# Two-layer MLP after attention on one core: the first block's first part with plain products, token operands made in the last group of the part before, bank evictions ahead of weights

## The chip, the cores and the metric

The kernel runs on one core of a Trainium2 chip. The metric is device time in microseconds (us) of one execution. TensorE (PE in the profile) multiplies, ScalarE (ACT), VectorE (DVE) and GpSimd (POOL) do elementwise work, SyncE (SP) issues the DMA transfers.

## The reference, cut to what matters

Causal attention with a decay comes first (4 batches, 8 heads, 576 tokens of 64 values). Its output, 2304 tokens of 512 values, goes through two gated layers:

```python
def _moe_ref(x, w_gate, w_val, w_out, rms_g):          # 512 -> 1536 -> 512
    rms = np.sqrt(np.mean(x * x, axis=-1, keepdims=True) + 1e-06)
    xn = x / rms * rms_g
    g = xn @ w_gate
    silu = g * (1.0 / (1.0 + np.exp(-g)))
    val = xn @ w_val
    return silu * val @ w_out

def _moe2_ref(x, w_in, w_out):                         # 512 -> 2048 -> 512
    h = x @ w_in
    g = h * (1.0 / (1.0 + np.exp(-h)))
    return g @ w_out
```

The weights arrive as 64-bit floats, the tokens as 32-bit floats, and the result is 32-bit.

## The kernel before

Attention is the same in both kernels. It ends with a normalisation of the tokens, which are kept in SBUF in the buffer `xa`, features on the partitions. Behind it come layer **a** (gate, val, out) and layer **b** (in, out). Each runs over two parts of the tokens: part 0 has 1280 tokens (two tiles of 512 and a rest of 256), part 1 has 1024 (two tiles of 512). The stages below are called a0, a1, b0 and b1.

Every 32-bit product is made of three matmuls on TensorE, since both operands are split into a rounded high part and a remainder (`terms`: high x high, high x low, low x high). A split is one copy on ScalarE (names that end in `h`: `wh`, `b11h`, `hh`) and one subtraction on VectorE (`wl`, `b11l`, `hl`).

A stage is a loop over groups of two hidden blocks of 128 (six groups in layer a, eight in layer b). A group does the following:

- It loads each weight matrix's two blocks (`unit_in`). In part 0 they come as raw 64-bit words (`st`) and are converted by one ScalarE and four VectorE operations (lines 128 to 132), and a copy of the result is kept in DRAM; in part 1 that copy is read back (`f<-kepta`).
- It multiplies by seven products instead of eight (Strassen's scheme over 2 x 2 blocks: two feature halves and two token tiles, `Products`): p1, p2, p6, p5, p7, p4, p3, each of 6 matmuls of 512 columns, so 42 per weight matrix. The weight sums that it needs are made on POOL (line 147), and the token operands are `b11`, `b21`, `t2`, `t1`, `t3`, `t4`, `b22`. In part 0 the 256 `rest` tokens follow at the end, as plain products (24 matmuls of 256 columns per matrix).
- The finished sums are taken out of the PSUM banks by `copy` (line 632, ScalarE, tile `c`) and `plus` (line 636, VectorE); gate and val are multiplied, split (`hh`, `hl`) and wait for the output product.
- The output product of a group (`second1` at line 742, `second2` at line 759) runs inside the next group, between the products, and adds its banks (`s`) into `xa`.

The token operands are made by `prepare(ph)` (lines 583ff.), which is called at the head of a part's first group: four differences on POOL (line 588, 128x1024 each, in the weight buffers `f`), seven or eight splits on ScalarE and VectorE (lines 579 and 580).

What order an engine's instructions have is decided by a scheduler from the order of the code, its dependences and the hint in `spread`, which lets a group's weight work start behind a marked instruction of the group before. The pools bound how far anything runs ahead: four `wh`/`wl` buffers, two `st` and two `f`, eight `c` tiles, two `s` and six `t` banks. Each engine runs its instructions in the order that came out, so one that waits holds those behind it.

## Time and profile before

| | |
|---|---|
| median of 3 runs | 1115.4 us (1111.41 to 1116.17) |
| the profiled execution | 1112.8 us, of which its span 1111.0 us |
| busy: PE, DVE, ACT, POOL | 1044.0, 803.7, 600.6, 413.2 us (94, 72, 54, 37% of the span) |
| mean granted TensorE clock | 0.972 |
| chain of work that ended last | PE 63%, DVE 17%, ACT 7%, POOL 6%, issue 5%, DMA 2% |
| costliest groups off PE | POOL `f` line 147 120.1 us, DVE `wl` line 151 99.8, DVE `hl` line 580 98.0, DVE `xa` line 759 86.6 |

The span runs from the first to the last instruction of one profiled execution; the time has some 2 us more around it. A matmul's own duration in the profile overlaps the next one's, so what a matmul costs is read from the distance of starts in a stretch without waits.

### The profile page before, as it was taken

To read this page: it belongs to the slowest core of one execution; us is meant where nothing else is said; L and a number is where in the kernel's file an instruction comes from. 1 tells how busy PE (TensorE), PEld (TensorE's weight loads), DVE (VectorE), ACT (ScalarE), POOL (GpSimd) and SP (SyncE) were. 2 spreads that over 40 slices of the span, in tenths; PEclk is the share of its full clock that TensorE was granted. 3 is DMA by queue.
4 is the path that set the end of the run, shared out by engine and by line. 5 is a ranking of instruction groups with operands and counts; after the bars stand their busy time and mean duration, and the time that the engine had idled before them with its cause. 6 is when DMAs were issued, how large, how long until landed. Compare 5 with 4: busy or idle time off the path is not lost.

```text
span 1111.0 us, 15986 instructions
## 1 busy us (share of the span) xinstructions
PE 1044.0 (94%) x5403; PEld 847.2 (76%) x5403; DVE 803.7 (72%) x1540; ACT 600.6 (54%) x1215; POOL 413.2 (37%) x631
## 2 busy tenths in 40 slices
PE   8998999968999999997999999799999999999998
PEld 7766778746787787785778888578888877888887
DVE  7788787866777888866546568877888897456664
ACT  7888888755554444443454344465454555544441
POOL 7766667503224214226423433422122243221310
PEclk9989999987999999998999999899999998999999
DMA  6644333110425225221111111133333313311202
GB/s 139 172 132 106 86 87 89 31 58 1 137 90 171 86 86 171 76 67 42 63 48 48 58 58 57 46 126 123 123 125 125 124 45 101 108 39 51 71 13 76
DMA packets 108402, 95.92 MB, mean 86 GB/s; under 512 B 62256, under 2 KB 83152, under 8 KB 108320
## 3 DMA queue, kind: packets, MB, share of 16 engines
q1 hardware_dynamic: 108320, 94.89, 28.2%
q8 instruction: 43, 0.70, 0.3%
q14 instruction: 39, 0.32, 0.1%
HBM read 72.25 MB, written 22.62 MB: 85 GB/s over the span
## 4 chain that ended last, share of the span: by engine, by line
PE 63%; DVE 17%; ACT 7%; POOL 6%; issue 5%; DMA 2%; POOLq 0%; SPq 0%; DVEq 0%; ACTq 0%
PE t L621 25%; PE s L621 23%; PE s L406 5%; PE t L429 4%; PE o L457 3%; POOL f L147 3%; DVE wl L151 3%; POOL f L588 2%; ACT wh L150 2%; DVE hl L580 1%; DVE c L131 1%; DVE xa L759 1%; PE s L365 1%; DVE c L636 1%; DMA f<-kepta 1%
## 5 line engine op out<-in xcount | busy, mean ns | idle before, releaser
L147 POOL TENSOR_TENSOR f<-f 128x256 f32<-128x256 f32 x160 | 120.1, 772 | 319.5 <-DVE f L132 85.7
L162 POOL TENSOR_TENSOR wol<-c,woh 128x512 fp32r<-128x512 f32 x56 | 74.9, 1348 | 214.3 <-ACT woh L161 210.7
L151 DVE TENSOR_TENSOR wl<-f,wh 128x1024 fp32r<-128x1024 f32 x80 | 99.8, 1256 | 55.1 <-ACT wh L150 55.1
L580 DVE TENSOR_TENSOR hl<-c,hh 128x512 fp32r<-128x512 f32 x140 | 98.0, 705 | 55.4 <-ACT hh L579 54.3
L632 ACT ACTIVATE c<-t 128x512 f32<-128x512 f32 x120 | 69.9, 590 | 101.0 <-PE t L621 100.0
L150 ACT ACTIVATE wh<-f 128x1024 fp32r<-128x1024 f32 x80 | 79.3, 999 | 72.1 <-POOL f L147 56.3
L636 DVE TENSOR_TENSOR c<-t,c 128x512 f32<-128x512 f32 x120 | 81.6, 686 | 49.6 <-ACT c L632 32.7
L621 PE MATMUL s<-woh,hh 128*128 128x512 f32 x290 | 114.1, 393 | 2.4 <-DVE xa L759 2.4
L579 ACT ACTIVATE hh<-c 128x512 fp32r<-128x512 f32 x140 | 81.4, 584 | 62.7 <-POOL c L713 44.5
L621 PE MATMUL s<-wol,hh 128*128 128x512 f32 x290 | 113.1, 390 | 0.0
L621 PE MATMUL s<-woh,hl 128*128 128x512 f32 x290 | 113.0, 390 | 0.0
L759 DVE TENSOR_TENSOR xa<-s,xa 128x512 f32<-128x512 f32 (+1 forms) x127 | 86.6, 682 | 32.6 <-PE s L621 32.1
L706 ACT ACTIVATE c<-c 128x512 f32<-128x512 f32 x84 | 52.8, 629 | 94.5 <-DVE c L636 94.5
L621 PE MATMUL s<-hh,woh 128*128 128x512 f32 (+1 forms) x240 | 90.3, 376 | 12.1 <-DVE xa L742 12.1
L393 POOL TENSOR_SCALAR dt<-ncb,c8t 128x64 f32<-128x64 f32 (+2 forms) x144 | 79.4, 553 | 41.2 <-DVE nm L409 32.7
L621 PE MATMUL s<-hl,woh 128*128 128x512 f32 (+1 forms) x240 | 89.4, 373 | 0.2 <-DVE hl L580 0.2
L621 PE MATMUL s<-hh,wol 128*128 128x512 f32 (+1 forms) x240 | 89.4, 373 | 0.0
L421 ACT ACTIVATE pr<-pr,nm 128x192 f32<-128x192 f32 (+3 forms) x144 | 80.1, 556 | 16.1 <-DVE nm L409 11.0
L409 DVE CUSTOM_DVE_ANT_0 pr<-s,dt 128x64 f32<-128x64 f32 (+7 forms) x160 | 70.2, 451 | 20.5 <-PE s L406 7.7
L742 DVE TENSOR_TENSOR xa<-s,xa 128x512 f32<-128x512 f32 (+1 forms) x100 | 62.4, 633 | 20.8 <-PE s L621 20.8
L429 PE MATMUL t<-ident,pr 128*128 128x128 f32 x384 | 72.2, 289 | 3.3 <-ACT pr L421 1.6
L621 PEld LDWEIGHTS s<-woh,hh 128*128 128x128 f32 x290 | 54.7, 189 | 17.2 <-DVE xa L759 6.6
(190 smaller groups left out, 2781.3 us busy)
## 6 DMA issues: line engine op xcount, KB each, us to landing
st<-in_moe_w_out_dram SPq DMA_DIRECT2D x28, 512.0 KB, 3.7
st<-in_moe_w_in_dram SPq DMA_DIRECT2D x16, 512.0 KB, 3.8
st<-in_moe_w_gate_dram SPq DMA_DIRECT2D x12, 512.0 KB, 3.9
kepta<-f SPq DMA_DIRECT2D x24, 256.0 KB, 2.2
st<-in_moe_w_val_dram SPq DMA_DIRECT2D x12, 512.0 KB, 3.9
f<-kepta SPq DMA_DIRECT2D x24, 256.0 KB, 2.6
out_dram<-xa SPq DMA_DIRECT2D x17, 256.0 KB, 2.0
ncb<-nc8d SPq DMA_DIRECT2D x30, 144.0 KB, 3.1
```

Of the source, the lines that this page charges most:

```text
L147: nc.gpsimd.tensor_tensor(out=out_, in0=x, in1=y, op=op)
L150: nc.scalar.activation(out=hi[i][:, u], in_=f[i][:, u], func=AF.Copy)
L151: nc.vector.tensor_tensor(out=lo[i][:, u], in0=f[i][:, u], in1=hi[i][:, u].bitcast(F32), op=ALU.subtract)
L162: nc.gpsimd.tensor_tensor(out=lo, in0=f, in1=hi.bitcast(F32), op=ALU.subtract)
L393: nc.gpsimd.tensor_scalar(out=dt, in0=p.nct[:, :n], scalar1=c8t[:, c, p.i : p.i + 1], scalar2=1.0, op0=ALU.add, op1=ALU.mult)
L421: e = nc.scalar.activation(out=pr, in_=pr, func=AF.Exp, bias=self.nm, scale=-1.0, accum_out=p.batch.sums[:, self.c, p.hp : p.hp + 1])
L429: nc.tensor.transpose(pt[:, jj * P : (jj + 1) * P], pr[:, jj * P : (jj + 1) * P], ident)
L579: nc.scalar.activation(out=hi, in_=src, func=AF.Copy)
L580: nc.vector.tensor_tensor(out=lo, in0=src, in1=hi.bitcast(F32), op=ALU.subtract)
L621: nc.tensor.matmul(ps, lhsT=l, rhs=r, start=start and z == 0, stop=stop and z == len(mms) - 1, skip_group_check=not (start and stop))
L636: nc.vector.tensor_tensor(out=t, in0=ps, in1=t, op=ALU.add)
L759: nc.vector.tensor_tensor(out=a, in0=ps, in1=a, op=ALU.add)
```

## The change

Five edits:

1. Layer a's part 0 multiplies plainly (`unit_plain`, `block`): for each 128 hidden units 12 matmuls of 512 columns per token tile, so 48 per weight matrix and group where there were 42. No weight sums are made, one tile holds both blocks of a matrix, and the low half of the weights is made on POOL. The buffers `b11`, `b21`, `t4`, `b22` hold the plain halves of the two token tiles there.
2. `prepare` gives back its pieces one by one. For the three later parts they are issued in the last group of the part before, each behind the product that last used the buffer it overwrites (`coming`), in pieces of 128x512; the differences go into `c` tiles. The first part's splits are written straight behind attention.
3. The evictions of the banks (`copy`, `plus`, `put`, the additions into `xa`) are put 600 places ahead in the scheduler's order.
4. In b0 the products of the 256 rest tokens are done behind p2 and behind p7 instead of at the end of the group.
5. In b0 the second half of the weights' low part goes to POOL, and the `c` ring has nine tiles instead of eight.

```diff
+AHEAD = 600
...
         for i in range(2):
             u = slice(0 if plain or not i else 1, 4)
             nc.scalar.activation(out=hi[i][:, u], in_=f[i][:, u], func=AF.Copy)
-            nc.vector.tensor_tensor(out=lo[i][:, u], in0=f[i][:, u], in1=hi[i][:, u].bitcast(F32), op=ALU.subtract)
+            (nc.gpsimd if plain and i else nc.vector).tensor_tensor(out=lo[i][:, u], in0=f[i][:, u], in1=hi[i][:, u].bitcast(F32), op=ALU.subtract)
...
+    def unit_plain(w, key, m):
+        w, s = words(w)
+        hi, lo = wip.tile([P, 4, G2], F32R, tag="wh", name="wh"), wip.tile([P, 4, G2], F32R, tag="wl", name="wl")
+        f = plain_half()
+        for i in range(2):
+            weights(f[:, 2 * i : 2 * i + 2].rearrange("p a f -> p (a f)"), w[:, s * (m + i) * P : s * (m + i + 1) * P], s * P, (key, m + i))
+        nc.scalar.activation(out=hi, in_=f, func=AF.Copy)
+        nc.gpsimd.tensor_tensor(out=lo, in0=f, in1=hi.bitcast(F32), op=ALU.subtract)
...
+        def diff(nm, u, v):
+            t[nm] = [tmp.tile([P, TT], F32, tag="c", name="c") for _ in range(2)]
+            for o, u_, v_ in zip(t[nm], u, v):
+                nc.gpsimd.tensor_tensor(out=o, in0=u_, in1=v_, op=ALU.subtract)
+        def parts_(nm, src):
+            for c in range(2):
+                split(xs[nm][0][:, c], xs[nm][1][:, c], src[c])
+        def p6():
+            diff("t1", b[0, 1], b[0, 0])
+            diff("t2", b[1, 1], t["t1"])
+            parts_("t2", t["t2"])
...
         def copy(ps):
             t = tmp.tile([P, TT], F32, tag="c", name="c")
-            nc.scalar.activation(out=t, in_=ps, func=AF.Copy)
+            with tc.high_priority(offset=AHEAD):
+                nc.scalar.activation(out=t, in_=ps, func=AF.Copy)
             return t
...
+        if plain:
+            where = [[(xs[nm], c) for nm in pr for c in range(2)] for pr in (("b11", "b21"), ("t4", "b22"))]
+            where.append([(xs["rest"], c) for c in range(NCC)])
+            def block(n, i, j):
+                w = TT if j < 2 else CUT - 2 * TT
+                ps = bank(pst)[:, :w]
+                terms(ps, [(win[n][i][c], [t[:, c_] for t in x]) for c, (x, c_) in enumerate(where[j])], True, True)
+                put(n, (i, j), ps, w)
+            return [(f"tile{j}" if i else "", [_p(block, n, i, j) for n in range(len(win))]) for j in (0, 1, 2) for i in range(2)]
...
-            order += [_p(s.rest, i) for i in range(2) for s in sets]
+            order.insert(5, ("rest", [_p(s.rest, 1) for s in sets]))
+            order.insert(2, ("", [_p(s.rest, 0) for s in sets]))
...
-            if g == 0:
-                prepare(ph)
+            coming = prepare(parts_left.pop(0)) if g + G >= NF and parts_left else {}
...
+            for nm, ps in order:
+                for p in ps:
+                    p()
+                for fn in todo[: 2 if len(ps) == 2 else 1 + (len(todo) > 7)]:
+                    fn()
+                    todo.remove(fn)
+                coming.pop(nm, int)()
...
+    parts_left = [1, 0, 1]
+    for j, names in enumerate((("b11", "b21"), ("t4", "b22"))):
+        for i, nm in enumerate(names):
+            for c in range(2):
+                split(xs[nm][0][:, c], xs[nm][1][:, c], xparts[0][:, 2 * i + c, j * TT : (j + 1) * TT])
...
     for ph in range(2):
-        layer("a", [w_gate, w_val], w_o1, second1, ph)
+        layer("a", [w_gate, w_val], w_o1, second1, ph, ph == 0)
```

Line numbers of the changed kernel are higher: the conversion's VectorE lines 129 to 132 are its 131 to 134, the split's 580 is 593, the addition into `xa` is 798 in layer a (742 before) and 816 in layer b (759), the multiplication of gate and val 760 (713).

First place: VectorE at the end of attention. In the kernel before, the sums of squares (`u`, line 282, then `ms`, line 286) stand between the last conversion steps of two output-weight blocks (`c_4078`, `c_4092`).

```order
L131 SCALAR_TENSOR_TENSOR c_4078<-st_4079,c_4078 128x512
L130 TENSOR_SCALAR c_4092<-c_4092 128x512
L132 SCALAR_TENSOR_TENSOR c_4078<-st_4079,c_4078 128x512
L282 TENSOR_TENSOR u_3915<-s_3909,r_3902 128x4x4 x2
L282 TENSOR_TENSOR u_3915<-s_3909,r_3902 64x4 x2
L131 SCALAR_TENSOR_TENSOR c_4092<-st_4093,c_4092 128x512
L284 TENSOR_TENSOR u_3915<-u_3915,r_3902 128x40
L132 SCALAR_TENSOR_TENSOR c_4092<-st_4093,c_4092 128x512
L286 TENSOR_REDUCE ms_3916<-u_3915 128x5
```

In the changed kernel the rows from the last scaling of the tokens (line 340) on are these, with the conversion of the same two blocks (`c_4080`, `c_4094`):

```order
L340 SCALAR_TENSOR_TENSOR xa_60<-xa_60,gcol_96,s_3973 128x288
L593 TENSOR_TENSOR b11l_3991<-xa_60,b11h_3990 128x512 x2
L593 TENSOR_TENSOR b21l_3993<-xa_60,b21h_3992 128x512 x2
L593 TENSOR_TENSOR t4l_4001<-xa_60,t4h_4000 128x512 x2
L593 TENSOR_TENSOR b22l_4003<-xa_60,b22h_4002 128x512 x2
L593 TENSOR_TENSOR restl_4011<-xa_60,resth_4010 128x512 x2
L131 TENSOR_SCALAR c_4080<-c_4080 128x512
L131 TENSOR_SCALAR c_4094<-c_4094 128x512
L132 TENSOR_SCALAR c_4080<-c_4080 128x512
L132 TENSOR_SCALAR c_4094<-c_4094 128x512
L133 SCALAR_TENSOR_TENSOR c_4080<-st_4081,c_4080 128x512
```

The conversion has moved from ahead of the normalisation to behind the first part's splits, which are one run now.

Second place: VectorE where one group of a0 follows another. Before, the second matrix's raw conversion (`f_5524`, `f_5525`) of the next group, the additions of output banks `s` and the remainder of the weights (`wl`) stand like this:

```order
L129 TENSOR_SCALAR f_5524<-f_5524 128x512
L129 TENSOR_SCALAR f_5525<-f_5525 128x512
L580 TENSOR_TENSOR hl_5485<-c_5468,hh_5484 128x256
L130 TENSOR_SCALAR f_5524<-f_5524 128x512
L130 TENSOR_SCALAR f_5525<-f_5525 128x512
L131 SCALAR_TENSOR_TENSOR f_5524<-st_5526,f_5524 128x512
L131 SCALAR_TENSOR_TENSOR f_5525<-st_5535,f_5525 128x512
L132 SCALAR_TENSOR_TENSOR f_5524<-st_5526,f_5524 128x512
L132 SCALAR_TENSOR_TENSOR f_5525<-st_5535,f_5525 128x512
L742 TENSOR_TENSOR xa_60<-s_5598,xa_60 128x512
L742 TENSOR_TENSOR xa_60<-s_5606,xa_60 128x512
L151 TENSOR_TENSOR wl_5521<-f_5524,wh_5520 128x1024
```

In the changed kernel, at the like place:

```order
L760 TENSOR_TENSOR c_5495<-t_5497,c_5495 128x512
L131 TENSOR_SCALAR f_5778<-f_5778 128x512
L798 TENSOR_TENSOR xa_60<-s_5515,xa_60 128x512
L593 TENSOR_TENSOR hl_5512<-c_5495,hh_5511 128x512
L798 TENSOR_TENSOR xa_60<-s_5523,xa_60 128x512
L132 TENSOR_SCALAR f_5778<-f_5778 128x512
L131 TENSOR_SCALAR f_5778<-f_5778 128x512
L133 SCALAR_TENSOR_TENSOR f_5778<-st_5779,f_5778 128x512
L132 TENSOR_SCALAR f_5778<-f_5778 128x512
L134 SCALAR_TENSOR_TENSOR f_5778<-st_5779,f_5778 128x512
L133 SCALAR_TENSOR_TENSOR f_5778<-st_5788,f_5778 128x512
L134 SCALAR_TENSOR_TENSOR f_5778<-st_5788,f_5778 128x512
```

The additions (line 798) stand among the steps of the conversion instead of behind all eight of them (`f_5778` is one tile of two blocks, so its rows come twice), and no `wl` follows, since it is made on POOL.

Third place: VectorE where b1 follows b0. Before, in the first group of b1, the additions of output banks (line 759), the token operands (`b11l`, `b21l`, `t1l`) and the weights' remainders (`wl`) stand in this order:

```order
L636 TENSOR_TENSOR c_9608<-t_9626,c_9608 128x512
L759 TENSOR_TENSOR xa_60<-s_9639,xa_60 128x512
L580 TENSOR_TENSOR b11l_3997<-xa_60,b11h_3996 128x1024
L759 TENSOR_TENSOR xa_60<-s_9647,xa_60 128x512
L580 TENSOR_TENSOR hl_9636<-c_9608,hh_9635 128x512
L151 TENSOR_TENSOR wl_9795<-f_9798,wh_9794 128x1024
L759 TENSOR_TENSOR xa_60<-s_9663,xa_60 128x512
L151 TENSOR_TENSOR wl_9797<-f_9799,wh_9796 128x768
L580 TENSOR_TENSOR b21l_3999<-xa_60,b21h_3998 128x1024
L759 TENSOR_TENSOR xa_60<-s_9678,xa_60 128x512
L580 TENSOR_TENSOR t1l_4003<-f_9824,t1h_4002 128x1024
```

In the changed kernel the same operands stand in the last group of b0:

```order
L816 TENSOR_TENSOR xa_60<-s_9571,xa_60 128x512
L593 TENSOR_TENSOR b11l_3991<-xa_60,b11h_3990 128x512
L816 TENSOR_TENSOR xa_60<-s_9579,xa_60 128x512
L593 TENSOR_TENSOR hl_9568<-c_9536,hh_9567 128x512
L593 TENSOR_TENSOR b11l_3991<-xa_60,b11h_3990 128x512
L593 TENSOR_TENSOR b21l_3993<-xa_60,b21h_3992 128x512 x2
L816 TENSOR_TENSOR xa_60<-s_9610,xa_60 128x512
L153 TENSOR_TENSOR wl_9767<-f_9770,wh_9766 128x1024
L153 TENSOR_TENSOR wl_9769<-f_9771,wh_9768 128x768
L816 TENSOR_TENSOR xa_60<-s_9626,xa_60 128x512
L593 TENSOR_TENSOR t2l_3995<-c_9638,t2h_3994 128x512
L593 TENSOR_TENSOR t2l_3995<-c_9639,t2h_3994 128x512
```

The token operands come in pieces of half the size, one group earlier, with the additions (line 816) between them.

## Rows read from the trace of the kernel before

**Rows 1.** Chain that ended last, in order of time: start, us, engine, line.

```profile
345.55 2.72 PE s L621 x12
356.43 1.43 PE s L621 x12
```

**Rows 2.** Eight stretches: us, busy of PE, PEld, DVE, ACT, POOL; clock, DMA.

```profile
251.06:295.20 44.14, 38.00 (x160) 30.47 (x160) 32.28 (x45) 21.20 (x33) 15.17 (x10) 0.85 0.14 45
295.20:459.10 163.90, 155.43 (x809) 130.92 (x807) 131.33 (x213) 75.95 (x130) 43.73 (x48) 1.00 0.35 114
459.10:540.00 80.90, 69.05 (x310) 56.21 (x311) 52.52 (x66) 32.52 (x48) 36.81 (x31) 0.92 0.24 78
540.00:660.86 120.86, 118.64 (x523) 96.41 (x522) 69.62 (x89) 54.93 (x86) 43.77 (x45) 1.00 0.14 44
660.86:736.60 75.74, 66.08 (x287) 53.09 (x285) 59.45 (x82) 35.89 (x56) 29.54 (x23) 0.95 0.24 77
736.60:877.41 140.81, 139.05 (x660) 114.87 (x661) 114.87 (x190) 76.98 (x135) 29.11 (x31) 1.00 0.36 117
877.41:940.00 62.59, 58.60 (x265) 48.19 (x266) 54.52 (x69) 33.95 (x54) 26.28 (x21) 0.95 0.26 86
940.00:1107.74 167.74, 167.67 (x745) 138.73 (x743) 98.00 (x131) 71.74 (x119) 35.61 (x38) 1.00 0.19 62
```

**Rows 3.** The same columns, for layer a's first stretch and one later group.

```profile
251.06:257.80 6.74, 6.51 (x16) 4.59 (x16) 6.74 (x9) 2.72 (x3) 2.14 (x1) 0.50 0.01 2
375.50:417.30 41.80, 39.34 (x204) 33.17 (x204) 34.29 (x57) 18.08 (x30) 11.20 (x13) 1.00 0.34 113
```

**Rows 4.** What PE waited for, 240 to 1111 us: total, times, longest.

```profile
PE t L621 <- ACT c L632: 13.1, 4, 5.9
PE s L621 <- DVE xa L742: 12.1, 7, 4.2
PE t L621 <- ACT wh L150: 11.7, 8, 3.4
```

**Rows 5.** PE's timeline where it waits: start, us, instruction, idle before and releaser.

```profile
265.30 0.79 PE L621 MATMUL t<-t2h,wh 128*128 128x512 f32 x1 [3.63 <-ACT c L632]
...
375.93 0.50 PE L621 MATMUL s<-hh,woh 128*128 128x512 f32 x1 [1.28 <-DVE xa L742]
...
378.77 0.50 PE L621 MATMUL t<-b11h,wh 128*128 128x512 f32 x1 [1.17 <-ACT wh L150]
...
527.43 0.72 PE L621 MATMUL s<-hh,woh 128*128 128x512 f32 x1 [4.17 <-DVE xa L742]
...
700.64 0.80 PE L621 MATMUL t<-t4h,wh 128*128 128x512 f32 x1 [5.90 <-ACT c L632]
```

**Rows 6.** VectorE's timeline at the end of attention.

```profile
240.08 1.60 DVE L131 SCALAR_TENSOR_TENSOR c<-st,c 128x512 int32<-128x512 int32 x1
...
241.71 0.69 DVE L132 SCALAR_TENSOR_TENSOR c<-st,c 128x512 int32<-128x512 int32 x1
...
243.16 1.27 DVE L297 TENSOR_TENSOR z<-y 128x5 f32<-128x5 f32 x1
...
244.86 0.17 DVE L297 TENSOR_TENSOR z<-y 128x5 f32<-128x5 f32 x1
```

**Rows 7.** PE's timeline behind it, up to layer a's first product.

```profile
246.78 0.74 PE L318 MATMUL s<-identr,rt 128*16 128x128 f32 x5 [7.04 <-DVE rt L309]
```

**Rows 8.** VectorE's timeline in the first group of b1: token operands.

```profile
912.85 1.21 DVE L580 TENSOR_TENSOR b21l<-xa,b21h 128x1024 fp32r<-128x1024 f32 x1
...
914.59 2.78 DVE L580 TENSOR_TENSOR t1l<-f,t1h 128x1024 fp32r<-128x1024 f32 x1
```

**Rows 9.** Groups by shape: weight splits and token differences; count, busy, mean ns.

```profile
L151 DVE TENSOR_TENSOR wl<-f,wh 128x1024 fp32r<-128x1024 f32 x60 | 74.0, 1242 | 53.2 <-ACT wh L150 53.2
...
L150 ACT ACTIVATE wh<-f 128x1024 fp32r<-128x1024 f32 x60 | 62.6, 1052 | 68.6 <-POOL f L147 54.4 <-PE t L621 14.2
...
L588 POOL TENSOR_TENSOR f<-xa 128x1024 f32<-128x1024 f32 x8 | 19.9, 2488 | 9.4 <-DVE wl L151 5.3 <-DVE t2l L580 2.5 <-DVE xa L327 1.4
```

More of the change, by code (lines that the diff above doesn't have):

```diff
@@ L653, in p2 @@
                 self.product(ps, "a12", "b21", True, True)
[L654 removed]
+                put(self.n, (0, 0), plus(ps, self.u1), TT)
             def p6(self):
@@ L719, in layer @@
             todo, pending[:] = list(pending), []
-            order = group(win, out_, ph == 0)
-            per = len(w_ins)
-            for i, p in enumerate(order):
-                p()
-                if i % per == per - 1:
-                    for fn in todo[: 2 if per == 2 else 1 + (len(todo) > 7)]:
-                        fn()
-                        todo.remove(fn)
+            order = group(win, out_, ph == 0, plain)
+            if plain and coming:
+                for nm in ("p6", "p5", "p7"):
+                    coming.pop(nm)()
+                coming = dict(tile0=[coming[nm] for nm in ("p1", "p2")], tile1=[coming[nm] for nm in ("p4", "p3")])
+                coming = {nm: _p(lambda fns: [fn() for fn in fns], fns) for nm, fns in coming.items()}
+            for nm, ps in order:
[5 more added lines that the diff above has]
+                coming.pop(nm, int)()
+            for fn in coming.values():
+                fn()
             for fn in todo:
@@ L738, in block @@
             a = xparts[ph][:, o, t : t + w]
-            if first:
-                nc.scalar.activation(out=a, in_=ps, func=AF.Copy)
-            else:
-                nc.vector.tensor_tensor(out=a, in0=ps, in1=a, op=ALU.add)
+            with tc.high_priority(offset=AHEAD):
+                if first:
+                    nc.scalar.activation(out=a, in_=ps, func=AF.Copy)
+                else:
+                    nc.vector.tensor_tensor(out=a, in0=ps, in1=a, op=ALU.add)
         return [_p(block, o) for o in range(NCC)]
@@ L755, in block @@
                 a = accs[ph][:, t // P + s, cs]
-                if first:
-                    nc.scalar.activation(out=a, in_=ps, func=AF.Copy)
-                else:
-                    nc.vector.tensor_tensor(out=a, in0=ps, in1=a, op=ALU.add)
+                with tc.high_priority(offset=AHEAD):
+                    if first:
+                        nc.scalar.activation(out=a, in_=ps, func=AF.Copy)
+                    else:
+                        nc.vector.tensor_tensor(out=a, in0=ps, in1=a, op=ALU.add)
                 if last:
```

68 lines of the change are left out of this document (35 added, 33 removed).

## The prediction

> **What bounds the kernel now.** I read the chain that ended last first: in the layers it runs for long pieces from PE to PE, so TensorE sets the time there, and every gap in PE's row is time. Its unwaited pieces give the price of a matmul by the distance of starts: 12 of 512 columns take 2.72 us, 0.2267 each, and 12 of 256 columns 1.43 us, 0.119 each [rows 1].
>
> Then I cut the layers, from the first product at 251.06 us to the end of the last at 1107.74, into eight stretches [rows 2]. In the trace they hold 3114 matmuls of 512 columns (1680 in products, 1434 in outputs) and 636 of 256. At the prices above that is 705.9 + 75.7 = 781.6 us, and the stretches last 856.7, so 75.1 us are lost. Each stretch's length less its own matmuls gives the place (wide and narrow counted in each): first group of a0 44.1 - 30.9 (111 and 48) = **13.3**; rest of a0 163.9 - 151.9 (519 and 288) = **12.0**; from a0 to a1 80.9 - 61.2 (226 and 84) = **19.7**; a1 120.9 - 116.8 (509 and 12) = **4.0**; from a1 to b0 75.7 - 62.0 (261 and 24) = **13.7**; b0 140.8 - 136.7 (540 and 120) = **4.1**; from b0 to b1 62.6 - 54.9 (217 and 48) = **7.7**; b1 167.7 - 167.1 (731 and 12) = **0.6**. The reader is to see that steady a1 and b1 run at PE's pitch already, and that four places where a part begins lose 54 of the 75.
>
> What ends the waits says why. PE waited 13.1 us in four pieces for a copy of a bank (line 632), 12.1 us for the addition into `xa` (line 742), 11.7 us for the weights' high half (line 150) [rows 4]. At three part starts the wait is 3.63, 4.17 and 5.90 us [rows 5]: VectorE and ScalarE there hold the token splits and the raw conversion, and what empties PSUM queues behind them. The rest of the loss is slow clock: from 251.06 to 257.80 the granted clock is 0.50, the 1.2 GHz level, and the stretches with long waits have a mean of 0.85 to 0.95 [rows 2, 3]. So a gap costs again behind itself, and a gap that goes gives that back.
>
> **The change, part by part.** The profiled execution took 1112.8 us, of which 1111.0 is span; its time is 2.6 below the median of the three runs. The sum is made on the span.
>
> *Plain products in a0.* 6 groups x 2 matrices x 6 more matmuls = 72, x 0.2267 = **+16.3 us**, in PE's own row, with nothing to hide them. For this VectorE loses all `wl` of a0 and POOL gets them. In a steady group of a0 VectorE is busy 34.29 of 41.80 us and POOL 11.20 [rows 3]. Two `wl` of 1.24 us per matrix leave VectorE: 4 x 1.24 = 5 us a group [rows 9]. On POOL the nearest row of that size is a difference of 128x1024 at 2.49 us [rows 9], two a group, so 5 us come while the weight sums go: POOL stays near 10 of some 41 us. That work is covered by the group before, as now one buffer pair per matrix leaves the other two for the next group; without that cover it would be 2.49 + 1.05 us ahead of each group. The two waits at a steady group start, 1.28 for `xa` and 1.17 for `wh` [rows 5], go both: the additions no longer stand behind eight conversion steps, and the weights have their buffers a group early. The 12.0 us become 2.0.
>
> *Evictions ahead.* They stand now where their bank is full, so PE waits for a copy's or an addition's own length at most, mostly covered by the other banks. This price is in the stretches below and isn't counted twice.
>
> *Token operands in the last group of the part before.* The number of elements is the same, so VectorE and ScalarE have as much to do, in pieces of half the size, in a group that has slack elsewhere. From 877.41 to 940.00 VectorE is busy 54.52 of 62.59 us, and PE's own matmuls take 54.9 [rows 2]: VectorE would be at 99% of PE's pitch. It fits only because the splits no longer have to be done before the first products, and because they may be slower than they need be today: `b21l` takes 1.21 us and `t1l` of the same shape 2.78 [rows 8]. That stretch is the one that I trust least; of its 7.7 us I keep 2.0. From a0 to a1 (52.52 of 80.9 busy) I keep 2.5 of 19.7, from a1 to b0 (59.45 of 75.74) 3.3 of 13.7 [rows 2]. The bounds are none of it kept and all of it kept.
>
> The Trainium skill has a rule against this part (page "SBUF — State Buffer", section "Who interferes with whom"): a VectorE instruction with two inputs in SBUF and a GpSimd instruction that reads SBUF share one read port, which one of them holds for its whole instruction. The trace agrees so far: 2.78 us against 1.21 with a POOL difference beside it. By that rule the differences and the splits get in each other's way in the new place too; that is rival B below.
>
> *The first splits.* They must still wait for attention's end, and the first products run at the slow clock for 6.7 us as now (16 matmuls that take 3.6 us at full clock, so some 3 lost). There are no differences any more, so the wait of 3.63 us [rows 5] and those behind it go. I keep 4.0 of 13.3.
>
> *Rest products in b0 earlier, the low half of the second matrix half on POOL.* Each takes a wait of tenths from b0; the `wl` that moves is 1.24 us of VectorE a group. I keep 2.5 of 4.1. Of a1's 4.0 I keep 3.0 and of b1's 0.6 all, since nothing but the evictions' order differs there.
>
> *The end of attention.* PE idles 7.04 us before the normalisation's transposes [rows 7], for a chain of small VectorE operations. In it stand two conversion steps of 1.60 and 0.69 us, and one of 1.27 us which takes 0.17 when it comes again [rows 6]. The order of the change has the conversion behind the splits. The gain is at most 1.60 + 0.69 + 1.10 = 3.4, at least 0 if another engine's part of the chain ends last; I take **-3.2**, since parts of the small ones overlap.
>
> **Sum.** Kept: 4.0 + 2.0 + 2.5 + 3.0 + 3.3 + 2.5 + 2.0 + 0.6 = 19.9, so 75.1 - 19.9 = 55.2 us come back. 1111.0 - 3.2 - 55.2 + 16.3 = 1068.9 us of span, and with 1.8 around it 1070.7: **1071 us**, 4% faster than the median.
>
> **Rivals.**
>
> *B, the splits stay slow.* If differences and splits still meet, 14 half splits at each of three part ends take 2.78 / 2 = 1.39 us in place of 0.6, 11 us more of VectorE at each; with VectorE at 99% of PE's pitch from b0 to b1 and with slack at the two others, 6 to 25 us come through beyond what is kept: 1077 to 1096, I say 1088. For it: [rows 8] and the load from b0 to b1. Against it: halves leave room between them, and evictions now go ahead of them.
>
> *C, a0's waits stay.* The conversion of the first output weights stands behind the splits, so the two `st` buffers come free only some 15 us later than now, the loads behind them too, and a0 might never catch up. Then the 12.0 us remain and some 5 more at the first group: 1071 + 10 + 5 = 1086. Against it: with 41 us a group and one load in four us the backlog goes in a group or two.
>
> *D, slower.* Evictions 600 places ahead can starve the weights: every eviction that is ready goes ahead of `wh` and `wl`, the next group's first products come late by one of each, 1.05 + 1.24 = 2.3 us [rows 9], at 28 group starts (6, 6, 8 and 8) 64 us, which eats the 55 and leaves the 16: 1071 + 64 = 1135. It decides from (1115.4 - 1071) / 28 = 1.6 us a group start on. Against it: PE waits for `wh` only eight times in all now [rows 4], and the buffers let the weights be made well ahead.
>
> *E, nothing is left over.* All the kept losses but the slow start and the a1 part go: 19.9 - 7 = 13 less, about 1058.
>
> **How the numbers follow.** Forecast 0.66, with a range of its own of 1060 to 1082 (keeping 9 to 31 of the 75 us); E 0.05; B 0.16; C 0.08; D 0.05. The range reaches down to E's side, 1056, and up over B and C to 1094, which leaves D and the ends of the others out, about 0.15. A measurement of this kernel can tell 0.5%, 5.6 us. Faster by more than that: all but D and its neighbourhood, 0.93; within it 0.02; slower 0.05.
>
> **What the changed profile would show.** Right: 72 more matmuls on PE; no wait over 1 us at a part start; PE's row from 295 us to the end of a0 at pitch, 6 x (144 wide and 72 narrow) = 41.2 us a group; a granted clock over 0.98 from 300 us on; the conversion behind 260 us and the normalisation's gap near 4 us. Wrong by B: `t1l`, `t2l` or `b21l` halves over 1.2 us in the three last groups, and banks waited for there. By C: waits for `wh` at each group start of a0. By D: waits for `wh` and `wl` at group starts of a1 and b1, where today there are none of note. Wrong altogether it is if VectorE's load rises to PE's pitch in b0, where it is busy 114.87 of 140.81 us today [rows 2] and I count on that falling.

## The result and the profile after

The changed kernel took 1084.2 us in the median of four runs, against 1115.8 for the kernel before: ratio 0.9712, 95% interval 0.9651 to 0.9774. Three of its runs lie between 1078.45 and 1085.16; a disturbed fourth (2618.83 us), like one of 4250.29 us of the kernel before, is left out of the ratio. Measured again beside the last experiments, it gave 0.9706 (0.9674 to 0.9738). The profiled execution has a span of 1081.5 us.

The page of the profile after, part 1 (busy us, share of the span, instructions):

```profile
PE 1046.3 (97%) x5475; PEld 856.1 (79%) x5475; DVE 766.7 (71%) x1508; ACT 569.5 (53%) x1191; POOL 402.9 (37%) x599
```

PE has 72 matmuls more and is busy for 97% of the span instead of 94. These are four of nine stretches into which I cut its layers, with the columns of [rows 2]:

```profile
295.00:470.00 175.00, 175.00 (x909) 150.78 (x908) 122.14 (x193) 64.16 (x111) 47.10 (x32) 1.00 0.35 113
470.00:520.00 50.00, 48.96 (x261) 41.83 (x260) 29.10 (x45) 21.15 (x35) 12.72 (x13) 1.00 0.11 32
...
650.00:680.00 30.00, 23.56 (x92) 17.72 (x91) 24.89 (x31) 12.81 (x22) 21.22 (x15) 0.94 0.16 53
...
860.00:900.00 40.00, 34.96 (x157) 27.92 (x157) 35.20 (x45) 22.24 (x42) 24.39 (x20) 0.96 0.13 43
```

The first two are the steady groups of a0 and the change from a0 to a1: PE is busy without a gap for 175 us, and from a0 to a1 it loses 1.6 us, where [rows 2] had 12.0 and 19.7. The other two are the last groups of a1 and of b0: 9.6 of 30 and 8.0 of 40 us are lost. In the kernel before the same two groups lost 8.3 and 7.6, so nothing is gained there. What PE waited for, 240 to 1082 us, the first lines:

```profile
PE t L647 <- ACT c L659: 4.9, 3, 2.6
PE s L647 <- DVE xa L816: 4.8, 2, 2.7
PE s L331 <- DVE rt L322: 4.1, 1, 4.1
PE t L647 <- ACT wh L152: 2.8, 2, 2.3
PE s L647 <- DVE xa L798: 1.7, 1, 1.7
```

The addition into `xa` of layer a (line 798) has gone from 12.1 to 1.7 us, the copies of banks from 13.1 to 4.9, and `wh` from 11.7 to 2.8 and 0.8 [rows 4]. The gap ahead of the normalisation is 4.1 instead of 7.04 [rows 7]. PE's remaining large waits stand in the two last groups:

```profile
661.69 0.50 PE L647 MATMUL s<-hh,woh 128*128 128x512 f32 x1 [1.71 <-DVE xa L798]
...
669.71 0.50 PE L647 MATMUL t<-t4h,wh 128*128 128x512 f32 x1 [1.86 <-ACT c L659]
...
673.99 0.50 PE L647 MATMUL t<-t4h,wh 128*128 128x512 f32 x1 [2.63 <-ACT c L659]
...
885.11 0.50 PE L647 MATMUL s<-woh,hh 128*128 128x512 f32 x1 [2.73 <-DVE xa L816]
...
897.29 0.50 PE L647 MATMUL s<-woh,hh 128*128 128x512 f32 x1 [2.03 <-DVE xa L816]
```

### The profile page after: what moved, and what is told of

Read it like the earlier page. It is cut to its first block, busy times and chain, and to the rows that moved or that the text cites. A ratio compares the mean times of both kernels' runs of the same rounds, so it can differ in the third digit from the quotient of the medians.

```text
span 1081.5 us, 16000 instructions
## 1 busy us (share of the span) xinstructions
PE 1046.3 (97%) x5475; PEld 856.1 (79%) x5475; DVE 766.7 (71%) x1508; ACT 569.5 (53%) x1191; POOL 402.9 (37%) x599
## 4 chain that ended last, share of the span: by engine, by line
PE 58%; DVE 8%; issue 6%; POOL 5%; ACT 2%; DMA 1%; POOLq 0%; ACTq 0%; DVEq 0%
PE t L647 31%; PE s L647 24%; POOL f L149 2%; DVE wl L153 1%; DVE hl L593 1%; DMA f<-kepta 1%; DVE c L664 1%; POOL c L760 1%; POOL wol L175 1%; DVE xa L798 1%; ACT wh L152 1%; ACT hh L592 1%; PE o L470 1%; DVE xa L816 1%; PE t L442 1%
## 5 line engine op out<-in xcount | busy, mean ns | idle before, releaser
L175 POOL TENSOR_TENSOR wol<-c,woh 128x512 fp32r<-128x512 f32 x56 | 79.0, 1420 | 255.5 <-ACT woh L174 196.1
L149 POOL TENSOR_TENSOR f<-f 128x256 f32<-128x256 f32 x112 | 84.8, 778 | 210.7 <-DMA f<-kepta 82.7
L593 DVE TENSOR_TENSOR hl<-c,hh 128x512 fp32r<-128x512 f32 (+1 forms) x140 | 113.6, 819 | 51.2 <-ACT hh L592 50.5
L592 ACT ACTIVATE hh<-c 128x512 fp32r<-128x512 f32 (+1 forms) x140 | 79.8, 586 | 61.9 <-DVE c L760 24.6
L664 DVE TENSOR_TENSOR c<-t,c 128x512 f32<-128x512 f32 x84 | 57.6, 688 | 41.8 <-ACT c L659 28.2
L153 DVE TENSOR_TENSOR wl<-f,wh 128x1024 fp32r<-128x1024 f32 (+1 forms) x48 | 57.1, 1197 | 41.6 <-ACT wh L152 41.6
L753 ACT ACTIVATE c<-c 128x512 f32<-128x512 f32 x66 | 41.6, 631 | 81.5 <-DVE c L664 81.5
L152 ACT ACTIVATE wh<-f 128x1024 fp32r<-128x1024 f32 (+1 forms) x56 | 54.1, 976 | 55.0 <-POOL f L149 36.1
L659 ACT ACTIVATE c<-t 128x512 f32<-128x512 f32 x84 | 49.6, 590 | 60.4 <-PE t L647 60.2
```

Of the source, the lines that this page charges most:

```text
L149: nc.gpsimd.tensor_tensor(out=out_, in0=x, in1=y, op=op)
L175: nc.gpsimd.tensor_tensor(out=lo, in0=f, in1=hi.bitcast(F32), op=ALU.subtract)
L592: nc.scalar.activation(out=hi, in_=src, func=AF.Copy)
L593: nc.vector.tensor_tensor(out=lo, in0=src, in1=hi.bitcast(F32), op=ALU.subtract)
L664: nc.vector.tensor_tensor(out=t, in0=ps, in1=t, op=ALU.add)
```

## The experiments

Each profile was read in the same way: group by group, from its first product to the next group's first, less its own matmuls at 0.2267 and 0.119 us. The sums by stage are below, with the time of the first product of the layers and the ratio of times to the kernel before (95% interval). In a0 and a1 the steady groups, the first and the last tell more than the sum, so those that matter are named in the text.

| kernel | ratio | first product at | a0 | a1 | b0 | b1 | lost |
|---|---|---|---|---|---|---|---|
| before | 1 | 251.06 | 31.4 | 26.2 | 17.0 | 0.3 | 74.9 |
| changed | 0.971 (0.965 to 0.977) | 244.79 | 5.4 | 13.7 | 15.2 | 1.0 | 35.3 |
| changed, again | 0.971 (0.967 to 0.974) | 246.37 | 5.5 | 11.4 | 18.5 | 0.3 | 35.6 |
| 1 seven products in a0 | 1.000 (0.998 to 1.003) | 252.41 | 43.3 | 16.9 | 15.2 | 0.9 | 76.3 |
| 2 operands late | 0.970 (0.965 to 0.975) | 248.87 | 5.3 | 7.8 | 16.1 | 6.8 | 36.1 |
| 3 no eviction ahead | 0.971 (0.965 to 0.977) | 248.95 | 4.5 | 14.2 | 16.3 | 0.6 | 35.6 |
| 4 t3 earlier | 0.971 (0.967 to 0.976) | 248.87 | 5.3 | 16.7 | 12.1 | 1.5 | 35.6 |
| 5 plain products alone | 0.976 (0.973 to 0.979) | 243.08 | 4.5 | 16.0 | 19.7 | 4.1 | 44.2 |
| 6 low halves on VectorE | 0.968 (0.964 to 0.972) | 241.19 | 4.5 | 14.0 | 12.4 | 5.7 | 36.6 |
| 7 a pair for each block | 0.975 (0.971 to 0.979) | 240.92 | 10.0 | 14.8 | 19.7 | 0.3 | 44.8 |
| 8 differences on VectorE | 0.963 (0.959 to 0.967) | 244.74 | 5.4 | 10.0 | 8.6 | 3.5 | 27.5 |
| 9 plain, old weight path | 1.004 (1.001 to 1.006) | 249.26 | 32.1 | 13.6 | 18.4 | 0.3 | 64.5 |
| 10 pair for each block, two staging tiles | 0.983 (0.979 to 0.986) | 243.13 | 14.8 | 14.7 | 15.6 | 1.0 | 46.1 |
| 11 as 8, b0's weights earlier | 0.966 (0.964 to 0.969) | 244.88 | 5.3 | 11.2 | 10.3 | 3.5 | 30.3 |

The first product comes anywhere from 240.9 to 249.0 us in the eleven profiles with the plain products' weights. In eight of them (the changed kernel twice, runs 2, 3, 4, 5, 8 and 11) the instructions of PE, VectorE, ScalarE and POOL stand in the same order up to there, by operation, tile and shape, and it still comes from 243.1 to 249.0. What differs is the granted clock at places: these are 20 us of the changed kernel and the same 20 us of run 2, with the columns of [rows 2]. PE is busy in both and gets through 127 matmuls in one, 98 in the other.

```profile
210.00:230.00 20.00, 19.83 (x127) 14.09 (x129) 13.14 (x52) 13.98 (x41) 5.03 (x14) 1.00 0.01 2
```

```profile
210.00:230.00 20.00, 20.00 (x98) 13.91 (x99) 10.91 (x42) 10.67 (x32) 4.97 (x14) 0.74 0.01 1
```

So a difference of a few us in span between two profiles says nothing of the layers, and the lost time of the groups is compared instead. That this spread is also most of what is uncertain in a ratio is likely (the four runs of run 3 lie between 1077.8 and 1089.4), but not shown, since only one execution of each kernel was profiled. The first four shared one chip and its runs of the kernel before, then four, then 9, 11 and the changed kernel again, then 10.

**1. Everything but the plain products.**

```diff
-        layer("a", [w_gate, w_val], w_o1, second1, ph, ph == 0)
+        layer("a", [w_gate, w_val], w_o1, second1, ph)
```

The plain splits behind attention go with it: the first part's operands come from `prepare(0)` again, differences included.

> Layer a's part 0 goes back to the seven products; everything else is as in the changed kernel, whose span is 1081.5 us. Theory: the plain products pay for their 72 matmuls by free buffers and free queues. Without them 16.3 us of matmuls go, 3 us of attention come back (the weight sums of the first group stand in POOL's queue there, and ScalarE waits for them with attention's own rows behind), the wait for wh of some 1.2 us comes back at five group starts (6 us), the differences at the head of the first group (8 us), and the change from a0 to a1 loses like that from a1 to b0 (13 us where it is 1.6): 1081.5 - 16.3 + 3 + 6 + 8 + 11 = 1093 us of span. Rival: the gain in a0 came from the evictions' place alone; then the matmuls saved are a gain and the span is 1081.5 - 16.3 + 3 + 8 = 1076.

Measured: span 1113.9, ratio 1.0003. Without the plain products nothing of the gain is left, though their 72 matmuls are saved. The loss in a0 rises from 5.4 to 43.3 us (its groups lose 14.5, 7.4, 6.4, 3.8, 4.2, 7.0), more than the theory had. PE's waits say what for:

```profile
PE t L647 <- ACT wh L152: 11.9, 9, 3.2
PE t L647 <- DVE wl L153: 7.4, 11, 1.1
PE s L647 <- DVE xa L798: 4.9, 4, 2.6
```

The weights lead. The changed kernel waits 2.8 and 1.5 us at these lines, and 0.8 and 1.7 at the plain products' own (164 and 165).

**2. Token operands at the head of their own part again.**

```diff
-            coming = prepare(parts_left.pop(0)) if g + G >= NF and parts_left else {}
+            coming = {}
+            if g == 0 and (n, ph) != ("a", 0):
+                for fn in prepare(parts_left.pop(0)).values():
+                    fn()
```

> The token operands of the three later parts are made at the head of the part's own first group again (still in halves, through the c tiles); all else as in the changed kernel. Theory: the early place is what saved the change from a0 to a1 (19.7 us lost before, 1.6 now) and saved little at the two later changes (13.0 and 8.0 lost now, 13.7 and 7.7 before). So a0 to a1 loses 10 to 15 again and the others stay: span 1090 to 1095. Rival: the early place is worth the same at every change and something else eats it at the later two, then these grow as well, to 20 and 14, and the span is 1105.

Measured: no difference in time, 36.1 us lost instead of 35.3. Both theories fall. By groups, the loss only moves: the last groups of a1 and b0 lose 0.9 and 1.2 instead of 9.6 and 8.1, the first ones of b0 and b1 9.8 and 6.5 instead of 3.4 and 0.6. From a0 to a1 the early place is worth 3 us (first group of a1 3.1 instead of 0.1), not 18, as long as the evictions stand ahead; with neither of the two, in run 5, that group loses 9.7.

**3. No eviction ahead.**

```diff
-            with tc.high_priority(offset=AHEAD):
+            with nullcontext():
```

(at all five places)

> The evictions of the banks have no place ahead in the schedule; all else as in the changed kernel. Theory: the additions into xa come again behind conversion steps, so a0's group starts lose some 1.3 us each (5 of them) and the three changes of part 2 to 4 us more each: span 1094. Rival: with plain products there is room enough without it, span 1081 within 3.

Measured: no difference (35.6 us lost); a0's steady groups lose 0.1 each in both. The rival was right, with the operands in their early place.

**4. The difference t3 with t1 and t2.** In the last group of b0 the changed kernel shows a wait that goes through three queues (timelines of ScalarE, POOL and VectorE):

```profile
894.89 0.63 ACT L592 ACTIVATE t3h<-c 128x512 fp32r<-128x512 f32 x1 [4.88 <-POOL c L603]
...
890.21 3.40 POOL L149 TENSOR_TENSOR f<-f 128x256 f32<-128x256 f32 x4 [4.63 <-DMA f<-keptb]
893.57 2.53 POOL L603 TENSOR_TENSOR c<-xa 128x512 f32<-128x512 f32 x2
...
895.56 1.08 DVE L593 TENSOR_TENSOR t3l<-c,t3h 128x512 fp32r<-128x512 f32 x1 [3.46 <-ACT t3h L592]
896.56 0.68 DVE L816 TENSOR_TENSOR xa<-s,xa 128x512 f32<-128x512 f32 x1
```

t3's difference stands on POOL behind weight sums that wait for a load; ScalarE's copy waits for it, VectorE's remainder for the copy, and behind that stands the addition that PE waits for at 897.29. The edit takes the difference ahead of the sums:

```diff
         def p6():
             diff("t1", b[0, 1], b[0, 0])
             diff("t2", b[1, 1], t["t1"])
+            diff("t3", b[1, 1], b[0, 1])
...
         def p7():
-            diff("t3", b[1, 1], b[0, 1])
```

> One difference (t3) is written together with t1 and t2, so POOL has it ahead of the weight sums of the next part's first group instead of behind them; nothing else differs from the changed kernel. Queue theory: from b0 to b1 ScalarE waited 4.9 us for t3 while the weight sums waited for their load, and VectorE's additions stood behind t3's remainder; the wait of 2.0 us on PE at 897 us goes, that at 674 us shrinks, and the span is 1077 to 1079. Port theory: it is the length of the halves beside POOL's differences (1.3 to 2.1 us instead of 0.68) that holds the additions up; two more differences at the crowded place make it no better: 1081 to 1084.

Measured: the same time. b0's last group loses 6.0 instead of 8.1, but a1's 12.7 instead of 9.6. The queue theory is right about that one wait (t3's copy now waits 0.57 us for POOL instead of 4.88) and wrong about the sum.

**5. The plain products alone.** Parts 2 and 3 of the change undone together (the operands still come in halves through `c` tiles), and b0's rest products at the end of the group, its low halves on VectorE and eight tiles in the ring:

```diff
-            order.insert(5, ("rest", [_p(s.rest, 1) for s in sets]))
-            order.insert(2, ("", [_p(s.rest, 0) for s in sets]))
+            order += [("", [_p(s.rest, 0) for s in sets]), ("rest", [_p(s.rest, 1) for s in sets])]
...
-            (nc.gpsimd if plain and i else nc.vector).tensor_tensor(
+            nc.vector.tensor_tensor(
...
-    tmp = ctx.enter_context(tc.tile_pool(name="tmp", bufs=9, reuse_waits="tile"))
+    tmp = ctx.enter_context(tc.tile_pool(name="tmp", bufs=8, reuse_waits="tile"))
```

> Only the plain products of layer a's part 0 are left of the change (with the first part's splits that belong to them): operands are made at the head of each part, evictions have no place ahead, b0's rest products stand at the end, all its low halves are on VectorE, and the ring has eight tiles. Theory: the plain products are the whole change, since without them nothing was left of the gain; span 1080 to 1088, ratio to before 0.97. Rival: the parts only work together; then the loss from a0 to a1 (20 us before) stays and the span is near 1097.

Measured: 0.976, some 27 us faster than before, with 44.2 us lost. So the plain products, with the weight path that belongs to them, hold most of the gain. What all the rest adds is some 0.5%, at the edge of what can be told: the intervals overlap a little, while all four times (1088.0 to 1091.0 us) lie above all eight of the changed kernel (1076.7 to 1086.2), which were taken beside other runs of the kernel before. The trace has it in the first groups of a1 and b0 (9.7 and 13.2 us lost).

**6. The low halves of a0's weights, and of all output weights, on VectorE.**

```diff
-        nc.gpsimd.tensor_tensor(out=lo, in0=f, in1=hi.bitcast(F32), op=ALU.subtract)
+        nc.vector.tensor_tensor(out=lo, in0=f, in1=hi.bitcast(F32), op=ALU.subtract)
```

(the same edit at lines 165 and 175). The second place, which the expectation does not name, is `unit_out`: all 56 `wol` of both layers move from POOL, where the middle one took 1.30 us, to VectorE, where it takes 0.68.

> As the changed kernel, but the low half of a0's weights is made on VectorE instead of POOL: two subtractions of 128x1024 a group (it was four in the kernel before). Load theory (a0 lost its time to a VectorE that was busy 82% of a group): 2.5 us a group come back on VectorE, and a0 with its change to a1 loses 5 to 10 us more than the 6 of the changed kernel. Buffer theory (the weights of a group could not be made before the group ahead had let its buffers go): nothing changes, a0 loses 4 to 6 us.

Measured: a0 loses 4.5 us, its steady groups 0.1 each, though VectorE got more work than was meant. VectorE's load is not what held a0 up.

**7. A pair of buffers for each block.**

```diff
-        hi, lo = wip.tile([P, 4, G2], F32R, tag="wh", name="wh"), wip.tile([P, 4, G2], F32R, tag="wl", name="wl")
+        hi, lo = zip(*((wip.tile([P, 4, G2], F32R, tag="wh", name="wh"), wip.tile([P, 4, G2], F32R, tag="wl", name="wl")) for _ in range(2)))
...
-        nc.scalar.activation(out=hi, in_=f, func=AF.Copy)
-        nc.gpsimd.tensor_tensor(out=lo, in0=f, in1=hi.bitcast(F32), op=ALU.subtract)
+        for i in range(2):
+            nc.scalar.activation(out=hi[i][:, :2], in_=f[:, 2 * i : 2 * i + 2], func=AF.Copy)
+            nc.gpsimd.tensor_tensor(out=lo[i][:, :2], in0=f[:, 2 * i : 2 * i + 2], in1=hi[i][:, :2].bitcast(F32), op=ALU.subtract)
```

> As the changed kernel, but each block of a0's weights has its own wh/wl pair, half of it used: a group takes all four buffers, as the seven products did, and the next group's weights cannot be made before this group's products let go. The copies and subtractions are of half size and twice as many. Buffer theory: PE waits for wh and wl at each of five group starts, 2 to 3 us each, and a0 loses 15 to 20 us instead of 5; span near 1095. Load theory: POOL and ScalarE have time, a0 loses 5 to 7.

Measured: a0 loses 10.0 us, but not where the buffer theory said: the steady groups lose 0.1 each, the first 3.0 and the last 6.1. Free wh/wl pairs alone are not the cause either.

**8. The differences on VectorE.**

```diff
-                nc.gpsimd.tensor_tensor(out=o, in0=u_, in1=v_, op=ALU.subtract)
+                nc.vector.tensor_tensor(out=o, in0=u_, in1=v_, op=ALU.subtract)
```

> As the changed kernel, but the differences t1 to t4 are made on VectorE instead of POOL, 8 of 0.68 us for each of the three parts. Port theory: the halves take 0.68 us instead of 1.3 to 2.1 since POOL reads nothing beside them, no engine waits for another's queue, and the last groups of a1 and b0 lose 3 to 5 us each instead of 9.6 and 8.1; span some 10 us lower. Load theory: VectorE's own work is what the last group can't hold, 5.4 us more of it make each of the two lose 12 to 14.

Measured: ratio 0.963, the fastest of all, 27.5 us lost. POOL's differences in the last group of b0 of the changed kernel, four of them merged into two lines:

```profile
878.79 3.44 POOL L603 TENSOR_TENSOR c<-xa 128x512 f32<-128x512 f32 x2
882.20 3.39 POOL L603 TENSOR_TENSOR c<-xa,c 128x512 f32<-128x512 f32 x2
```

The lines of VectorE's splits between 868 and 900 us (count, shortest/middle/longest ns), first of the changed kernel, then of this one:

```profile
L593 DVE TENSOR_TENSOR b11l<-xa,b11h x2: 676/1226/1777, 876.4 to 879.3; 128x512 fp32r<-128x512 f32 x2
L593 DVE TENSOR_TENSOR b21l<-xa,b21h x2: 1746/1759/1772, 881.0 to 882.7; 128x512 fp32r<-128x512 f32 x2
...
L593 DVE TENSOR_TENSOR t3l<-c,t3h x2: 1078/1231/1384, 895.6 to 897.2; 128x512 fp32r<-128x512 f32 x2
```

```profile
L593 DVE TENSOR_TENSOR b11l<-xa,b11h x2: 675/676/678, 873.0 to 875.8; 128x512 fp32r<-128x512 f32 x2
L593 DVE TENSOR_TENSOR b21l<-xa,b21h x2: 677/678/679, 876.4 to 877.0; 128x512 fp32r<-128x512 f32 x2
...
L593 DVE TENSOR_TENSOR t3l<-c,t3h x2: 676/676/677, 889.0 to 892.7; 128x512 fp32r<-128x512 f32 x2
```

The halves that took up to 1.78 us beside POOL's differences take 0.68 without them. b0's last group loses 1.1 instead of 8.1 us (b1's first 3.2 instead of 0.6). Though VectorE has 5.4 us more to do at each change of part, it is done sooner, so the load theory is out. Of the port theory the length of the halves is shown. That the 7.8 us less lost come from it alone is not: the edit also takes the differences out of POOL's queue, where those of t3 and t4 stood behind weight sums, and run 4 took only t3 out of it. a1's last group falls only from 9.6 to 6.6.

**9. Plain products with the old weight path.**

```diff
-            win = [spread(*((unit_plain, w, f"{n}{z}", g) if plain else (unit_in, w, f"{n}{z}", g, ph == 0))) for z, w in enumerate(w_ins)]
+            win = [spread(*(unit_in, w, f"{n}{z}", g, ph == 0)) for z, w in enumerate(w_ins)]
...
-                terms(ps, [(win[n][i][c], [t[:, c_] for t in x]) for c, (x, c_) in enumerate(where[j])], True, True)
+                terms(ps, [([t[:, c % 2] for t in win[n][f"a{i + 1}{c // 2 + 1}"]], [t[:, c_] for t in x]) for c, (x, c_) in enumerate(where[j])], True, True)
```

> Layer a's part 0 multiplies plainly as in the changed kernel, but its weights come the old way: two staging tiles and all four wh/wl pairs a group, the four sums made on POOL and split along (nothing reads them). This parts the two halves of the plain edit. Weight-path theory: the chain from freed pair over split, freed staging tile, conversion of the second matrix, sums and split (some 12 us in the trace of the kernel before) is what made the group starts late; then a0 loses 20 to 40 us here and the span is 1098 to 1115. Product theory: it was the seven products themselves (six copies and six additions out of banks a group, sums that later products continue) that lost the time; then a0 loses under 10 and the span is 1080 to 1088.

Measured: span 1115.2, ratio 1.0037: the whole gain is gone. The plain products are all there, a0 loses 32.1 us instead of 5.4, and PE waits 18.1 us for `wh`. The chain in the group that begins at 372.35 us, on ScalarE, VectorE, POOL and PE:

```profile
365.29 1.06 ACT L152 ACTIVATE wh<-f 128x1024 fp32r<-128x1024 f32 x1 [1.42 <-PE t L647]
...
366.73 1.06 ACT L152 ACTIVATE wh<-f 128x1024 fp32r<-128x1024 f32 x1
...
370.30 0.69 ACT L130 ACTIVATE f<-st 128x512 f32<-128x512 f32 x1 [1.95 <-POOL wl L153]
...
375.18 0.68 DVE L134 SCALAR_TENSOR_TENSOR f<-st,f 128x512 int32<-128x512 int32 x1
...
375.94 2.89 POOL L149 TENSOR_TENSOR f<-f 128x256 f32<-128x256 f32 x4 [5.67 <-DVE f L134]
...
378.06 2.01 ACT L152 ACTIVATE wh<-f 128x1024 fp32r<-128x1024 f32 x2 [4.22 <-POOL f L149]
...
379.17 0.50 PE L647 MATMUL t<-b11h,wh 128*128 128x512 f32 x1 [2.78 <-ACT wh L152]
```

Gate's first split waits until PE lets a buffer go (365.29). Gate's weights are split (to 370.27), which frees a staging tile; only then val's second block is converted (to 375.86), then come the sums (to 378.83) and val's split. PE is at val's first product 2.78 us earlier. In the changed kernel one staging tile holds a whole matrix, and at the like group change, at 359.79 us, val's split had been done at 344:

```profile
332.49 2.41 POOL L165 TENSOR_TENSOR wl<-f,wh 128x1024 fp32r<-128x1024 f32 x1 [7.42 <-ACT wh L164]
341.74 2.40 POOL L165 TENSOR_TENSOR wl<-f,wh 128x1024 fp32r<-128x1024 f32 x1 [6.84 <-ACT wh L164]
```

**10. A pair for each block and two staging tiles, no sums.** To run 7 it adds a staging tile for each block:

```diff
-        f = plain_half()
+        f = [plain_half() for _ in range(2)]
```

> Plain products, all four wh/wl pairs a group (as in the run that gave each block its own pair), and now also two staging tiles a matrix, but no sums: between that run and the one with the whole old weight path it differs by the staging alone. Staging theory: val's conversion waits for gate's split as in the kernel before, 4.9 us of conversion and 2 of split then stand between, and PE waits 1 to 3 us at each of five group starts; a0 loses 15 to 30. Sums theory: without the 2.9 us of sums the chain just fits under the group's end, and a0 loses 5 to 12 as with one staging tile.

Measured: a0 loses 14.8 us, 10.8 of them in its last group (5.9 there on an addition into `xa`), and its steady groups 0.1 each. In the steady groups neither the buffers (run 7) nor the buffers with two staging tiles (here) cost anything; with the sums, and the splits of twice the width that go with them (run 9), 3.3 to 5.3 us a group are lost. Sums and wider splits were not parted.

**11. Run 8 with b0's first weights one mark earlier.**

```diff
-            after = marks[min(LEAD[i], len(marks) - 1)]
+            after = early[0] if early else marks[min(LEAD[i], len(marks) - 1)]
...
+            early[:] = prior[-1:] if (n, g, ph) == ("b", 0, 0) else []
             win = [spread(
...
+            prior[:] = marks
```

> Differences on VectorE as in the run before of that kind, and the first weights of b0 may start one mark earlier (behind the last activation of the group before a1's last), so that their conversion is done before t2's split. Theory: in a1's last group ScalarE's wh waited 3.5 us for POOL's sums, which waited for the conversion's last step between the token splits, and copies of banks stood behind wh: of the 6.6 us lost there 3 go, span 1070 to 1072, ratio 0.960. Rival: it is VectorE's sum of work in that group, and moving its order only moves the wait: ratio 0.963 as before.

Measured: 0.966, not told apart from run 8. The wait is still there, on ScalarE in the last group of a1:

```profile
666.43 2.00 ACT L152 ACTIVATE wh<-f 128x1024 fp32r<-128x1024 f32 x2 [3.31 <-POOL f L149]
```

The rival's number came, but its cause, VectorE's sum of work, was not tested: the last step of the conversion ends 2.45 us earlier than in run 8 (662.62 instead of 665.07 us), POOL's sums take 4.44 us instead of 2.92, and the split on ScalarE starts only 0.9 us earlier. Beside it stood the changed kernel again, with this expected of it:

> The changed kernel unaltered, beside the two others on one chip, to place them: ratio to before 0.968 to 0.974 if the first measurement holds.

It held.

## Why the prediction was right, and where its steps failed

The forecast was 1071 us, the range 1056 to 1094, and 1084.2 was measured: inside the range, but above the likeliest case's own 1060 to 1082, at the place of rival B. The sum of the terms missed by 13 us of span, and behind the sum the credit was given to the wrong part. The direction and the places in a0 came from the mechanism; that the time still fell inside the range owes as much to the range's width of 38 us. Of the signs named ahead, a0's pitch (41.3 us a group for 41.2) and the gap near 4 us came, and so did that of rival B, `b21l` halves of 1.75 us with banks waited for.

**Plain products.** The +16.3 us are there: 72 matmuls at pitch. That the steady waits of a0 vanish was right (0.1 us a group; the 12.0 us became 0.4 plus a backlog of 3.2 in the second group). Why they vanish I had wrong: without the spare buffers the steady groups run at pitch too (runs 7 and 10), and the relief of VectorE that I counted beside them does nothing (run 6). What counts is the shorter chain to the weights: with the old path, plain products and all, the loss is back (run 9), by its sums or its wider splits, on top of the buffers and the staging. Mis-sized above all: I gave this edit 10 of the 55 us, and 9 more in the first group, where its differences go. With everything else kept, taking it back costs 41.0 us of lost time (76.3 against 35.3, run 1), and alone it brings the loss from 74.9 to 44.2 (run 5).

**Token operands in the last group of the part before.** This is the step that failed. I had 33 us come back at three changes of part (19.7 to 2.5, 13.7 to 3.3, 7.7 to 2.0). At the two later changes nothing came back: 13.0 and 8.7 us are lost in the last and first groups (9.6 + 3.4 and 8.1 + 0.6) where I kept 3.3 and 2.0. That is 16.4 us, more than the whole miss. The kernel before shows why there was little to move: its VectorE makes b1's operands from 905.8 to 931.4 us, and PE's first product of b1 stands at 930.35 (VectorE's last operand and that product):

```profile
930.18 1.22 DVE L580 TENSOR_TENSOR b22l<-xa,b22h 128x1024 fp32r<-128x1024 f32 x1
...
930.35 0.40 PE L621 MATMUL t<-b11h,wh 128*128 128x512 f32 x1
```

So [rows 8] are not of the first group of b1, as I had them, but of PE's last group of b0: by the order of the code the operands came later, in time they were there already. For b0 four of seven splits (`b11l`, `b21l`, `t1l`, `t2l`) were likewise made before its first product (676 to 704 us, against 708.27). Run 2 shows the loss going where the work goes, 9.8 and 6.5 us in the first groups instead. Only from a0 to a1 did the splits of the differences come behind the first product in the kernel before (514 to 526 us, against 499.63), and there the loss did come back, 13.7 us to 0.1 in a1's first group. No single edit has the credit for that: the group loses 9.7 with plain products alone (run 5), 3.1 with all but the early place (run 2), 0.1 with all but the evictions ahead (run 3), and 2.1 with all but the plain products (run 1). The 7 us of a0's last group go with the plain products (7.0 in run 1, 0.1 in run 5).

**Rival B, the port.** I gave it 0.16 and its price was 6 to 25 us; 16 came at its two places, and run 8 takes 8 of them back. The rule of the Trainium skill that I had set against this part (page "SBUF — State Buffer", section "Who interferes with whom") is borne out: the halves took 1.08 to 1.78 us beside a POOL difference and 0.68 in run 8. I read [rows 8] too simply, though: the 1.21 us of `b21l` stand beside a POOL difference as well. That one began 0.22 us later and itself took 3.21 instead of 2.40:

```profile
909.71 2.40 POOL L588 TENSOR_TENSOR f<-xa 128x1024 f32<-128x1024 f32 x1 [3.59 <-DVE wl L151]
913.07 3.21 POOL L588 TENSOR_TENSOR f<-xa,f 128x1024 f32<-128x1024 f32 x1 [0.96 <-DVE wl L151]
```

In these rows the instruction that began first kept its length, and the other grew. Run 8 is faster at 0.963 than the change at 0.971 (its interval ends below that of the second measurement, made beside other runs); run 11, which has the same edit and stood beside that second measurement, has 0.966 against 0.971 with intervals that overlap. The port is not all: 6.6 us stay in a1's last group, where POOL has no differences any more.

**Evictions ahead.** I counted their gain in the stretches. Taken back alone, they are worth nothing that can be measured (run 3). With the operands late they seem to be worth something: a1's first group loses 3.1 with them (run 2) and 9.7 in run 5, which differs in the ring and in b0's edits too. Rival D, weights starved by them, did not happen: b1 loses 1.0 us.

**End of attention.** Expected -3.2; PE's gap fell from 7.04 to 4.06 us, so 3.0, by the conversion's new place, as forecast: the small VectorE operations now follow each other without it. The layers began 6.3 us earlier, not 3. One term I had not seen: the first group's weights are made inside attention. In the three profiles with the old weight path the first product comes at 249.3 to 252.4 us, in the eleven others at 240.9 to 249.0. The kernel before shows a reason at 53.84 us, a ScalarE `wh` that waits 2.28 us for POOL's sums with attention's own copies behind it. The two ranges nearly touch, and one order of instructions gives 243.1 to 249.0 by itself, so its size stays open.

**Rival C** came in small: the second group of a0 waits 0.83 us for `wh` and 1.70 for `wl`, 3.2 lost in all; the 12 us that it kept for a0 do not stay.

**Sum.** 1068.9 us forecast; 15.4 us more lost (35.3 for 19.9) and 3.1 less ahead of the layers make 1081.2, and the profile has 1081.5.

Open are four things: how much the rest of the change adds to the plain products (some 0.5%, hardly told apart), why the seven products lose even more in a0 with the rest of the change (43.3 against 31.4), which of sums and wider splits weighs more in run 9, and how much of run 8's gain is the port and how much POOL's queue.

## What to carry to other kernels

Before arithmetic is saved by a scheme that needs prepared operands, follow the preparation of the next operand from the buffer that it must wait for to the first instruction that reads it; in a0 that chain ended behind the group's end, and a plain scheme with a shorter chain bought back 41 us for 16 us more of matmuls. Before work is moved ahead of a boundary, look in the trace where it stands in time: an engine that runs ahead may do it there already, whatever the order of the code says. Then compare the lost time of both groups together, since the cost goes where the work goes. And where several edits come in one change, take each back alone and leave each standing alone, since the trace of the whole credits the one that is nearest to the gap, and of two edits that serve the same wait each looks worthless when it alone is taken back.

## What was not expected of the hardware

A subtraction of 128x512 on VectorE took 0.68 us, and up to 1.78 while POOL made a difference. The steps of the raw conversion that have a scalar for a second operand lengthened too: in the last group of a1 one took 1.51 us in the changed kernel, and 0.42 at the like place of run 8.

```profile
656.29 1.51 DVE L131 TENSOR_SCALAR f<-f 128x512 f32<-128x512 f32 x1
```

```profile
654.71 0.42 DVE L131 TENSOR_SCALAR f<-f 128x512 f32<-128x512 f32 x1
```

And the granted clock of the same instructions in the same order differed between executions: 1.00 in the changed kernel and 0.74 in run 2 from 210 to 230 us, with PE busy in both, which is where run 2's first product falls back by 4 us.
